# Transformer block (infini-attention and SwiGLU) on one core: first q and k by token quarters, and a table of priority shifts for the list scheduler

## The chip, the cores and the metric

The kernel runs on one core of a Trainium2 chip. The time is device microseconds of one execution. A run counts as fast when it is within 1.5% of the fastest of the same kernel. Differences in this study are below 1%, so next to the times I use a ledger of TensorE's own time, read from the trace matmul by matmul.

## The reference, cut to what matters

```python
x = A_x                                            # (1, 2048, 1024), bf16
h  = x + attention(layernorm(x), wq, wk, wv, wo, beta)   # 32 heads of 32
h2 = h + (silu(hn @ w1) * (hn @ w3)) @ w2                # hn = layernorm(h), F = 3584

# attention: 4 segments of 512 tokens, in order
for s in range(4):
    p   = softmax(qs @ ks.T * scale + mask)        # inside the segment
    mem = phi(qs) @ M / (phi(qs) @ z + 1e-6)       # from the segments before
    outs.append(g * mem + (1 - g) * (p @ vs))
    M, z = M + phi(ks).T @ vs, z + phi(ks).sum()
```

## The kernel before

The kernel builds a list of operations, each with a class, a place in the list (`seq`), dependences and a modelled cost. A list scheduler plays the list on a model of the engines and writes down an order for each engine; this order is what the chip runs. Each engine works through its order as written, so the scheduler decides who stands behind whom. A free engine takes the ready operation with the lowest (class, seq):

```python
def offer(o):
    o.offered = now
    for e in o.engs:
        heapq.heappush(avail[e], (o.cls, o.seq, o))
```

Matmuls of one accumulation form a group, which claims a PSUM bank when its first matmul is scheduled; from then on that matmul also depends on whoever had the bank last. A group marked `safe` asks for all its loads before its first matmul:

```python
if group.safe and group.ops:
    head = group.ops[0]
    for d, raw in list(o.deps.items()):
        if (not raw or d.kind == "dma") and d.seq < head.seq:
            self.dep(head, d, raw=raw)
```

Scores use one set of four banks, freed by one exponential on ScalarE (ACT). They run in a packed mode of TensorE (four matmuls of 32 rows); dense matmuls run in the full mode; the products with v in a column mode:

```python
def scores(self, s, parts):
    gr = self.queue(0, 1, 2, 3)
    ... 4 packed matmuls for each part, cls=0 ...
    self.g.op("act", act_ns(2048), ex, writes=[et[:, :, :]], cls=0, group=gr)   # exp
```

At the start, four row blocks of x are normalised, transposed on TensorE and copied to SBUF; the first q runs in two halves of 256 tokens so as not to wait for all four:

```python
def first_q(self, w):
    x = self.xnT[0]
    grs = [Group([(6,), (7,), (4,), (5,)], safe=True) for _ in range(4)]
    for half in range(2):
        c0 = 256 * half
        for i, gr in enumerate(grs):
            self.mms(gr, [(lambda gr, c0=c0: self.bank(gr, 0, 256, c0),
                           w[:, c, i * 128:(i + 1) * 128], x[:, c, c0:c0 + 256],
                           c == 0, c == 7, 256) for c in range(8)], 5, split=8, eager=True)
    for i, gr in enumerate(grs):
        self.evac(gr, self.qT[0][:, i, :], 512, lambda b: b, cls=1)
```

```python
self.g.dma(hr[:, :], self.hd[t * 128:(t + 1) * 128, :], cls=3)
...
gr = self.dense_group(True)                        # True: safe
self.mms(gr, [... 28 matmuls with hm[fc] and w2[fc // 4] ...], 8, eager=True)
self.g.op("dve", ..., reads=[hs], writes=[ob], cls=1, group=gr)   # ob = hs + bank
```

The softmax here doesn't subtract the row's maximum and nothing guards it: scores larger than these inputs give would overflow.

Of the kernel before, what the change touches and what calls it, by code (L numbers as in the profile page):

```python
# [13 lines left out]
ENGINES = ("pe", "act", "dve", "pool", "sp")  # L14


class Op:


    __slots__ = ("engs", "eng", "cost", "emit", "deps", "users", "cls", "seq", "missing",  # L20
                 "ready", "start", "end", "pos", "signal", "tok", "group", "first", "last",
                 "mode", "bytes", "kind", "snap", "gate", "port", "patience", "offered")

    def __init__(self, engs, cost, emit, cls, seq):
        self.engs, self.cost, self.emit, self.cls, self.seq = engs, cost, emit, cls, seq
        self.eng = None
        self.deps, self.users = {}, []
        self.missing = 0
        self.ready = 0.0
        self.start = self.end = None  # L30
        self.pos = None
        self.signal = False
        self.tok = None
        self.group = None
        self.first = self.last = False
        self.mode = None
        self.bytes = 0
        self.kind = None
        self.snap = None
        self.gate = None  # L40
        self.port = False
        self.patience = 0.0
        self.offered = 0.0


class Group:
# [23 lines left out]
class Graph:  # L70
# [9 lines left out]
    def __init__(self, nc, es):  # L80
        self.nc, self.es = nc, es
        self.ops = []
        self.pages = {}
        self.base = {}
        self.eng = {"pe": nc.tensor, "act": nc.scalar, "dve": nc.vector,
                    "pool": nc.gpsimd, "sp": nc.sync}
        self.bank_owner = [None] * 8
        self.bank_last = [[] for _ in range(8)]
        self.phase_left = {}


    def sbuf(self, name, shape, dtype, offset):
# [68 lines left out]
    def op(self, engs, cost, emit, reads=(), writes=(), cls=5, deps=(), group=None,  # L161
           kind=None, gate=None, port=False):
        if isinstance(engs, str):
            engs = (engs,)
        if not isinstance(cost, dict):
            cost = {e: cost for e in engs}
        o = Op(engs, cost, emit, cls, len(self.ops))
        o.kind = kind
        o.gate = gate
        o.port = port  # L170
        if gate is not None:
            self.phase_left[gate] = self.phase_left.get(gate, 0) + 1
        for ap in reads:
            self._touch(o, ap, False)
        for ap in writes:
            self._touch(o, ap, True)
        for d in deps:
            self.dep(o, d)
        o.group = group
        for group in (group.parts if isinstance(group, Both) else (group,) if group else ()):  # L180
            for prev in group.ops:
                if prev.engs != o.engs or o.engs != ("pe",):
                    self.dep(o, prev)
            if group.ops and o.engs == ("pe",):
                self.dep(o, group.ops[-1])
            o.first = not group.ops
# [5 lines that stand above are left out]
            group.ops.append(o)  # L192
            group.open += 1
        self.ops.append(o)
        return o
# [11 lines left out]
    def dma_t(self, out, in_, cls=5):  # L207
# [3 lines left out]
        o.bytes = 2 * 262144  # L211
        return o


    def schedule(self):
        ops = self.ops
        for o in ops:
            o.missing = len(o.deps)
            for d in o.deps:
                d.users.append(o)  # L220
# [250 lines left out]
class Kernel:  # L471
# [218 lines left out]

    def ln_act(self, k, src, dst):

        sm, nm, sq = (self.lnst[:, k, i:i + 1] for i in range(3))
        junk = self.oT[0][:, 0:2, :].rearrange("p a b -> p (a b)")
        G = self.g
# [13 lines left out]

    def ln(self, k, src, dst, cls):  # L710

        st = self.lnst[:, k, :]
        mv = self.lnmv[:, k, :]
        for c in range(2):
# [14 lines left out]
    def ln1(self, s):  # L729
        for i in range(4):  # L730
# [7 lines left out]
            if s:  # L738
# [6 lines left out]
            self.evac(gr, out, 1024, lambda b: b.rearrange("p (k n) -> p k n", k=8), cls=1,  # L745
                      bf=True)

    def qkv(self, s):
        p = s % 2
        for half in range(2):  # L750
            for kind in "qkv":
                n = self.n_wp
                self.n_wp += 1
                w = self.wp[n % 3]
                src = self.w[kind][:, half * 512:(half + 1) * 512].rearrange(
                    "(c p) n -> p c n", p=128)
                if n == 0:
                    self.g.dma(w[:, :, 0:256], src[:, :, 0:256], cls=1)
                    self.g.dma(w[:, :, 256:512], src[:, :, 256:512], cls=1)
                else:  # L760
                    self.g.dma(w[:, :, :], src, cls=1)
                if n == 0:
                    self.first_q(w)
                    continue
                for i in range(4):
                    gr = self.dense_group()
                    if kind == "v":
                        items = [(lambda gr: self.bank(gr), self.xnT[s][:, c, i * 128:(i + 1) * 128],
                                  w[:, c, :], c == 0, c == 7, 512) for c in range(8)]
                        out = self.v[p][:, i, half * 4:half * 4 + 4, 0:128]  # L770
                        view = lambda b: b.rearrange("p (g n) -> p g n", g=4)
                    else:
                        items = [(lambda gr: self.bank(gr), w[:, c, i * 128:(i + 1) * 128],
                                  self.xnT[s][:, c, :], c == 0, c == 7, 512) for c in range(8)]
                        out = (self.qT if kind == "q" else self.kT)[p][:, half * 4 + i, :]
                        view = lambda b: b
                    self.mms(gr, items, 5)
                    self.evac(gr, out, 512, view, cls=1)

    def first_q(self, w):  # L780

        x = self.xnT[0]
        grs = [Group([(6,), (7,), (4,), (5,)], safe=True) for _ in range(4)]
        for half in range(2):
            c0 = 256 * half
            for i, gr in enumerate(grs):
                self.mms(gr, [(lambda gr, c0=c0: self.bank(gr, 0, 256, c0),
                               w[:, c, i * 128:(i + 1) * 128], x[:, c, c0:c0 + 256],
                               c == 0, c == 7, 256) for c in range(8)], 5, split=8, eager=True)
        for i, gr in enumerate(grs):  # L790
            self.evac(gr, self.qT[0][:, i, :], 512, lambda b: b, cls=1)

    def phi(self, src, dst, cls):
        n = self.n_phi
        self.n_phi += 1
        e_, r = self.pe_e[0][:, :, :], self.pe_r[0][:, :, :]
# [14 lines left out]
    def memory(self, s, pr):  # L811

        p = s % 2
# [2 lines left out]
        self.phi(self.kT[p][:, 2 * pr:2 * pr + 2, :], pk[:, :, :], 4)  # L816
        pkn = self.pkn[pr % 2]
        self.g.dma_t(pkn[:, :, :], pk[:, :, :].rearrange("p a n -> p (a n)"), 3)
        gr = self.dense_group()
        items = []  # L820
        for a in range(2):
# [36 lines left out]
    def scores(self, s, parts):  # L858


        q, k = self.qT[s % 2], self.kT[s % 2]
        et = self.et[self.n_et % len(self.et)]
        self.n_et += 1
# [44 lines left out]
    def finish(self, s, g, pq, pieces):  # L908


        G = self.g
        v = self.v[s % 2]
        pm = (s - 1) % 2
        gm = self.queue(4) if s else None
# [13 lines left out]
        else:  # L928
            order = [(w, kc) for kc in range(4) for w in "nd"]
        both = Both(gn, gd)  # L930

        def emit(e, gr):
            ins = []
# [47 lines left out]
    def wo_stage(self, s):  # L981
        oT = self.oT[s % 2]
        for i in range(4):
            t = 4 * s + i
            h, hn = self.h[t % 3], self.hn[0]
            self.g.dma(h[:, :], self.x2d[t * 128:(t + 1) * 128, :], cls=2)
            for half in range(2):
                gr = self.dense_group(s >= 2)
                self.mms(gr, [(lambda gr: self.bank(gr), oT[:, c, i * 128:(i + 1) * 128],
                               self.wo[:, c, half * 512:(half + 1) * 512], c == 0, c == 7, 512)  # L990
                              for c in range(8)], 5 if s < 2 else 7)
                hs = h[:, half * 512:(half + 1) * 512]
                self.g.op("dve", dve_ns(512), lambda e, gr, hs=hs: [e.tensor_tensor(
                    hs, hs, self.bank(gr), op=ALU.add)], reads=[hs], writes=[hs], cls=1,
                    group=gr)
# [2 lines left out]
            self.g.dma_t(self.hnT[s][:, :, i * 128:(i + 1) * 128], hn[:, :], 2)  # L998

    def ffn_up(self, blk, ch):  # L1000
        n = self.n_w13
        self.n_w13 += 1
        w1, w3 = self.w13[n % 2]
# [3 lines left out]
        for jj in range(2):  # L1007
            fc = 2 * ch + jj
            for tc in range(2):
                hT = self.hnT[2 * blk + tc]  # L1010
                i = self.n_f % 2
                self.n_f += 1
# [18 lines left out]
    def ffn_down(self, blk):  # L1031
# [4 lines left out]
        for i in range(8):  # L1036
            t = 8 * blk + i
            hr = self.hr[t % 3]
            self.g.dma(hr[:, :], self.hd[t * 128:(t + 1) * 128, :], cls=3)
            cols = [(0, 512), (512, 256), (768, 256)] if t == 15 else [(0, 512), (512, 512)]  # L1040
            for c0, n in cols:
# [98 lines left out]
```

## Time and profile before

| | before |
|---|---|
| time, median of 3 runs | 913.40 us (913.02 to 914.52) |
| profiled span | 911.39 us |
| TensorE busy | 902.3 us, 99% |
| next busiest engine, VectorE | 434.3 us, 48% |
| matmuls, changes of tiling mode in the order | 5500, 209 |

A busy share of 99% says that TensorE is the bound, but not how much of its time is needed. The ledger does. I walked the matmuls in order of start. Each start-to-start distance is its columns at 2.4 GHz, plus 2.5 ns, plus 0.117 us if the mode changes, plus a rest; a rest over 0.06 us is a stall. In some traces 93 or 94 matmul records are missing, so every trace was first aligned with the order of the built program. The lines behind it are in the prediction.

### The profile page before, as it was taken

What the parts mean: (1) busy time and instruction counts of PE and PEld (TensorE: products, weight loads), DVE (VectorE), ACT (ScalarE), POOL (GpSimd) and SP (SyncE); (2) the same over time, 40 slices, a digit from 0 to 9 for tenths busy, and PEclk for the clock granted to TensorE, in tenths of its full rate; (3) what the DMA queues carried; (4) which work ended last, traced back from release to release, by engine and by line L of the source; (5) the groups of instructions that cost most, each with busy time, mean ns of one, the idle gap of its engine ahead of it and who ended that gap; (6) DMA issues with size and microseconds to landing.
All of it is one profiled execution on the core that took longest, in us unless ns stands there. A gap on an engine that the chain in (4) does not pass through costs nothing.

```text
span 911.4 us, 13038 instructions
## 1 busy us (share of the span) xinstructions
PE 902.3 (99%) x5500; PEld 406.1 (45%) x5500; DVE 434.3 (48%) x744; ACT 293.7 (32%) x310; POOL 175.0 (19%) x272
## 2 busy tenths in 40 slices
PE   8999999999999999999999999999999999999998
PEld 5444444444444344444444444444444444444445
DVE  3878878878767654544643411211343334431111
ACT  5877775776776611111111100000121111110000
POOL 3535655555454520100100000000000000000000
PEclk9999999999999999999999999999999999999999
DMA  9967753743543255823733211012133212301110
GB/s 313 243 173 188 174 137 100 186 132 94 137 107 104 71 203 155 190 65 104 191 74 93 66 51 47 24 37 79 49 96 93 70 46 70 93 24 41 35 42 29
DMA packets 145385, 96.26 MB, mean 106 GB/s; under 512 B 45360, under 2 KB 132528, under 8 KB 145328
## 3 DMA queue, kind: packets, MB, share of 16 engines
q1 hardware_dynamic: 145328, 95.45, 38.3%
q8 instruction: 43, 0.70, 0.3%
q14 instruction: 14, 0.11, 0.0%
HBM read 76.55 MB, written 8.39 MB: 93 GB/s over the span
## 4 chain that ended last, share of the span: by engine, by line
PE 97%; ACT 2%; DVE 1%; DMA 0%; issue 0%; SPq 0%
PE ps L598 90%; PE ps L939 4%; PE ps L871 3%; ACT et L884 1%; DMA xs<-in_A_x_dram 0%; DVE lnst L716 0%; DVE qT L622 0%; PE ps L610 0%; DVE xs L725 0%; SPq L203 0%; ACT v L621 0%; ACT qT L621 0%; DVE ob L1050 0%; DVE xs L707 0%; DVE lnmv L718 0%
## 5 line engine op out<-in xcount | busy, mean ns | idle before, releaser
L598 PE MATMUL ps<-hnT,w1b 128*128 128x512 bf16 x896 | 223.3, 379 | 0.3 <-DVE t L1022 0.3
L598 PE MATMUL ps<-hnT,w3b 128*128 128x512 bf16 x896 | 222.6, 379 | 0.0
L1019 ACT ACTIVATE sg<-ps 128x512 bf16<-128x512 f32 x112 | 66.9, 597 | 438.3 <-PE ps L598 434.7
L598 PE MATMUL ps<-w2b,hm 128*128 128x512 bf16 (+1 forms) x924 | 196.4, 373 | 0.0
L1022 DVE SCALAR_TENSOR_TENSOR t<-sg,ps 128x512 bf16<-128x512 bf16 x112 | 76.9, 686 | 213.3 <-ACT sg L1019 213.3
L884 ACT ACTIVATE et<-ps 128x2048 bf16<-128x2048 f32 x80 | 150.0, 1875 | 45.3 <-PE ps L939 23.1
L598 PEld LDWEIGHTS ps<-w2b,hm 128*128 128x128 bf16 x924 | 90.4, 98 | 103.3
L598 PEld LDWEIGHTS ps<-hnT,w1b 128*128 128x128 bf16 x896 | 87.0, 98 | 106.8 <-issue 7.8
L598 PEld LDWEIGHTS ps<-hnT,w3b 128*128 128x128 bf16 x896 | 87.4, 98 | 105.8 <-issue 0.8
L889 POOL TENSOR_SCALAR_AFFINE_SELECT et<-et 128x512 bf16<-128x512 bf16 x128 | 89.5, 716 | 116.9 <-ACT et L884 116.5
L1027 DVE SCALAR_TENSOR_TENSOR hm<-t,ps 128x512 bf16<-128x512 bf16 x112 | 76.9, 686 | 34.4 <-PE ps L598 31.2
L1050 DVE TENSOR_TENSOR ob<-hr,ps 128x512 bf16<-128x512 bf16 (+1 forms) x33 | 22.1, 671 | 143.1 <-PE ps L598 143.1
L598 PE MATMUL ps<-hnT,wp 128*128 128x512 bf16 x256 | 61.9, 380 | 0.3 <-DVE qT L622 0.3
L598 PE MATMUL ps<-xnT,wp 128*128 128x512 bf16 (+1 forms) x288 | 61.1, 356 | 0.3 <-DVE qT L622 0.3
L598 PE MATMUL ps<-wo,oT 128*128 128x512 bf16 x256 | 59.9, 379 | 0.0
L598 PEld LDWEIGHTS ps<-xnT,wp 128*128 128x128 bf16 x288 | 26.1, 98 | 26.7 <-issue 4.1
L598 PEld LDWEIGHTS ps<-wo,oT 128*128 128x128 bf16 x256 | 24.2, 98 | 29.9 <-issue 2.3
L598 PEld LDWEIGHTS ps<-hnT,wp 128*128 128x128 bf16 x256 | 23.1, 98 | 29.3 <-issue 4.6
L976 POOL TENSOR_TENSOR Nm<-Nm,R1b 128x512 f32<-128x512 f32 x23 | 29.6, 1289 | 20.2 <-DVE R1b L965 20.2
L871 PE MATMUL ps<-qT,kT 32*128 32x128 bf16 (+3 forms) x512 | 31.7, 301 | 1.8 <-ACT et L884 1.7
L950 DVE STREAM_TRANSPOSE T<-ps 128x512 f32<-128x512 f32 x32 | 22.9, 715 | 21.8 <-PE ps L939 21.5
L598 PE MATMUL ps<-wp,hnT 128*128 128x512 bf16 x128 | 31.1, 380 | 0.0
(84 smaller groups left out, 590.4 us busy)
## 6 DMA issues: line engine op xcount, KB each, us to landing
w1b<-in_B_w_dram SPq DMA_DIRECT2D x28, 512.0 KB, 3.9
w3b<-in_B_w_dram SPq DMA_DIRECT2D x28, 512.0 KB, 4.6
wp<-in_A_wk_dram SPq DMA_DIRECT2D x8, 1024.0 KB, 6.6
wp<-in_A_wv_dram SPq DMA_DIRECT2D x8, 1024.0 KB, 5.6
wp<-in_A_wq_dram SPq DMA_DIRECT2D x7, 1024.0 KB, 5.5
w2b<-in_B_w_dram SPq DMA_DIRECT2D x7, 1024.0 KB, 8.1
xs<-in_A_x_dram SPq DMA_DIRECT2D x16, 256.0 KB, 5.5
h<-in_A_x_dram SPq DMA_DIRECT2D x16, 256.0 KB, 4.1
```

What stands on the lines that cost most here:

```text
L598: return [e.matmul(p[0](gr), p[1], p[2], start=p[3], stop=p[4]) for p in part]
L871: ins.append(e.matmul(self.bank(gr, j, 512 - 128 * kc, off), k[r, g, 128 * kc:128 * kc + 128], q[r, g, 128 * kc:512], start=True, stop=Tru ...
L884: return [e.activation(et[:, :, :], src, AF.Exp, scale=self.scale)]
L889: self.pool_op(lambda e, m=m: e.affine_select(m, m, pattern=[[0, 4], [1, 128]], compare_op=ALU.is_ge, fill=0.0, base=0, channel_multiplier ...
L939: ins.append(e.matmul(self.ps[r, b * 512 + 128 * kc:(b + 1) * 512], lhsT, pieces[kc][:, j, :], start=kc == 0 and (what == "n" or s == 0), ...
L950: G.op("dve", dve_ns(512), lambda e, gr: [e.transpose(T1, self.bank(gr))], writes=[T1], cls=0, group=gd)
L976: self.either(lambda e: e.tensor_tensor(Nm, Nm, R1, op=ALU.mult), 512, 2, [Nm, R1], [Nm], 2)
L1019: self.g.op("act", act_ns(512), lambda e, gr, sg=sg: [e.activation(sg, self.bank(gr), AF.Tanh, scale=0.5)], writes=[sg], cls=2, group=gg)
L1022: e.scalar_tensor_tensor(t1, sg, 1.0, self.bank(gr), op0=ALU.add, op1=ALU.mult)], reads=[sg], writes=[t1], cls=2,
L1027: e.scalar_tensor_tensor(dst, t1, 0.5, self.bank(gr), op0=ALU.mult, op1=ALU.mult)], reads=[t1], writes=[dst], cls=2,
L1050: self.g.op("dve", dve_ns(n), lambda e, gr, hs=hs, ob=ob, n=n: [e.tensor_tensor(ob, hs, self.bank(gr, 0, n), op=ALU.add)], reads=[hs], wri ...
```

## The change

The intent: TensorE should work sooner, on quarters of the tokens of which the rows are ready, for two groups of q and two of k; the values come third. Then the order of the whole attention should have fewer waits: a table, found by search with the scheduler's engine model, moves stages of the list earlier or later.

```diff
+SHIFT = {
+    0: (-342, 0), 1: (-212, 0), 2: (315, 0), 3: (-6, 1), 4: (101, 1), 5: (384, 0), 6: (-38, -1),
...                                   (467 entries: shift of seq, shift of class)
     def schedule(self):
         ops = self.ops
+        for o in ops:
+            late, cls = SHIFT.get(o.unit, (0, 0))
+            o.seq += late + 1e-6 * o.seq
+            o.cls += cls
...
+    def stage(self):
+        self.unit += 1                # called at each layer norm, group, score block, ...
...
-    def first_q(self, w):             # two halves of 256 tokens, four groups of q
...
+    def first_half(self):
+        (wq, sq), (wk, sk), (wv, sv) = (self.weights(kind, 0) for kind in "qkv")
+        self.g.dma(wq[:, :, 0:256], sq[:, :, 0:256], cls=1)
+        self.g.dma(wk[:, :, 0:256], sk[:, :, 0:256], cls=1)
+        self.g.dma(wv[:, :, :], sv, cls=1)
+        self.g.dma(wq[:, :, 256:512], sq[:, :, 256:512], cls=1)
+        self.g.dma(wk[:, :, 256:512], sk[:, :, 256:512], cls=1)
+        work = [(w, i, Group([(6,), (7,), (4,), (5,)], safe=True))
+                for w in (wq, wk) for i in range(2)]
+        for c0 in range(0, 512, 128):
+            for w, i, gr in work:
+                self.g.stage()
+                self.mms(gr, [(lambda gr, c0=c0: self.bank(gr, 0, 128, c0),
+                               w[:, c, i * 128:(i + 1) * 128], x[:, c, c0:c0 + 128],
+                               c == 0, c == 7, 128) for c in range(8)], 5, split=8, eager=True)
...                                   (copies; then v; then the other two groups of q and of k)
```

## The prediction

> **What bounds the kernel now.** I read the page's busy shares first, then its chain, then the merged chain in order of time, and last the TensorE timeline of the first 60 us.
>
> ```profile
> PE 902.3 (99%) x5500; PEld 406.1 (45%) x5500; DVE 434.3 (48%) x744; ACT 293.7 (32%) x310; POOL 175.0 (19%) x272
> PE 97%; ACT 2%; DVE 1%; DMA 0%; issue 0%; SPq 0%
> ...
> 330.21 578.62 PE ps L598 x2708
> ```
>
> TensorE is busy for 99% of the span and is 97% of the chain that ended last. No other engine passes 48%. The last line is the feed-forward part: 2708 matmuls in one piece, with nothing ahead of any of them. So only TensorE's own time counts, and I split it. The built program's order lists 5500 matmuls. Without the 16 warm-up ones (3.4 us of columns), and with the four packed ones of the attention counted as one, their columns are 860.2 us at 2.4 GHz: 809.0 in full mode, 17.1 in the scores' row mode, 34.1 in the column mode of the value product. That cannot change. What remains of the span of 911.4 is 51.2 us, in five terms:
>
> - A fixed cost of a matmul. In the last piece 2652 matmuls of 512 columns and 56 of 256 are 571.7 us of columns and took 578.62: 6.9 / 2708 = 2.5 ns each. Over the 3948 full-mode ones after the warm-up: 9.9 us.
> - Changes of tiling mode, 209 in the order. Their price is in the timeline:
>
> ```profile
> 22.02 0.40 PE L871 MATMUL ps<-qT,kT 32*128 32x512 bf16 x4
> 22.35 2.76 PE L598 MATMUL ps<-xnT,wp 128*128 128x512 bf16 x12
> 25.05 0.40 PE L871 MATMUL ps<-qT,kT 32*128 32x128 bf16 x8
> ```
>
> (Columns: start, duration, engine, line, tiles, count.) Four packed score matmuls are 0.213 us of columns, and the next starts 0.33 later; twelve dense ones are 12 x 0.2158 = 2.59, and the next starts 2.70 later. That is 0.11 to 0.12 for a change in either direction, and the median over the attention part is 0.117. 209 x 0.117 = 24.4 us.
>
> - The head, up to the dense stream:
>
> ```profile
> 1.24 6.40 PE L598 MATMUL ps<-oT 128*128 128x512 bf16 x16 [1.24 <-DVE oT L652]
> 7.48 0.61 PE L610 MATMUL ps<-ident,xs 128*128 128x128 bf16 x8
> 9.23 0.61 PE L610 MATMUL ps<-ident,xs 128*128 128x128 bf16 x8 [1.14 <-ACT xnT L621]
> 10.46 0.62 PE L610 MATMUL ps<-ident,xs 128*128 128x128 bf16 x8 [0.62 <-DVE xs L725]
> 11.04 1.03 PE L598 MATMUL ps<-xnT,wp 128*128 128x256 bf16 x8
> 11.91 0.61 PE L610 MATMUL ps<-ident,xs 128*128 128x128 bf16 x8
> 12.36 9.73 PE L598 MATMUL ps<-xnT,wp 128*128 128x256 bf16 x72
> ```
>
> By 12.36 us TensorE has done 4 transposes of eight (1.71 us of columns) and one block of the first q (0.85). So 9.8 us of the head are no useful work; the bracket on the transposes shows the cause, the layer norm of the rows.
>
> - Stalls inside the attention. Where a start-to-start distance exceeds columns, 2.5 ns each and the change of mode, the excess sums to about 4.2 us. Most hang on the one set of four score banks, which is free only when the exponential (1.88 us) has read it:
>
> ```profile
> 35.92 0.23 PE L939 MATMUL ps<-et,ones 128*32 128x128 bf16 x4
> 36.65 0.39 PE L871 MATMUL ps<-qT,kT 32*128 32x512 bf16 x4 [0.50 <-ACT et L884]
> 36.97 1.90 PE L598 MATMUL ps<-xnT,wp 128*128 128x512 bf16 x8
> 39.02 0.40 PE L871 MATMUL ps<-qT,kT 32*128 32x128 bf16 x8 [0.15 <-ACT et L884]
> ```
>
> 36.65 to 39.02 shows the shortest round of this loop: 2.37 us from scores to scores, with eight dense matmuls too few to fill it.
>
> - The tail after the last matmul, about 2.6 us (the piece above ends at 908.83).
>
> The sum is 9.9 + 24.4 + 9.8 + 4.2 + 2.6 = 50.9 of the 51.2.
>
> **What the Trainium skill says.** "TensorE: Matmul & The Clock Gate", Part 1, gives a warm start-to-start of N / 2.4 GHz plus about 2.5 ns; this trace agrees (2.5 ns over 2708). The same page, LDWEIGHTS, puts a weight load at columns over 1.2 GHz, 107 ns, and Weight-path perf modes names a faster load for full bf16 weights. It matters here, because the change halves the moving columns to 128. The trace shows eight matmuls of 129 columns, each with new weights, from 43.81 to 44.36: 0.55 less one change of mode is 0.43, or 54 ns each, so columns bound it and not the load. "TensorEngine Tiling (Array Packing)", Key Properties, says that changing the tiling mode drains TensorE; the 0.117 us agrees. "Perfetto Trace Analysis", Identifying the Most-Contended Engine, warns that matmul busy time is a bad measure, and so it is: 99% busy hides 51 us.
>
> **The change part by part.**
>
> 1. First q, k. Before, all four groups of the first q come in two halves of 256 tokens. After it, two groups of q and two of k come in four quarters of 128, in the same four banks. For the first q and k together, 64 matmuls of 256 columns and 32 of 512 become 128 of 128 and 32 of 512. Columns are equal; 64 more instructions cost 64 x 2.5 ns = +0.16 us. A block (8 x 54 ns) is 0.43 us and needs only its own quarter of the rows. The timeline with all engines has the first quarter's copy to SBUF end at 9.14 us (ACT, 8.12 plus 1.02), so a block can run before the second transpose. In the after order blocks stand ahead of transposes 2 and 3 and three ahead of transpose 4, five in all. DVE, ACT and GpSimd have the same order in the layer norm as before. From 9.25 on, TensorE has then 3 transposes and 5 blocks, 3.4 us, and passes transpose 4 at about 12.7, not 12.36. Work done by then: 5 x 0.43 = 2.15 against 0.85; gain 1.3 less the 0.34 later, 1.0 us. Seven to eight blocks follow, over 3 us, more than the last quarter's copy (1.1 us) needs, so no new gap. This is near the limit: of 9.23 to 12.36 only 1.0 us was idle, and what lies before 9.2 waits for the rows in both.
> 2. q and k halves loaded as 512 KB pieces, values third. The first slice moves 313 GB/s, so rows (1 MB), q and k halves (0.5 MB each) are there by about 8 to 9 us (estimate from that rate). The k half is first needed near 11. Nothing gained or lost by itself.
> 3. The table shifts the priority of some 467 units. It adds no instruction. By the order, the changes of mode go from 209 to 206: -0.35 us. I also added up, in both orders, columns, 2.5 ns and 0.117 us between score blocks and compared with 2.37 us. Before, six rounds are too short, by 3.1 us in sum (0.86, 0.2, 0.2 around 36 to 41 us, then 0.2, 0.84, 0.84); after, two, by 1.3 (1.06 early in the first segment, 0.2 later). The true stalls before were 4.2 because of waits for copies too (two of 0.33 on the qT copy). Taking the same 1.1 us for those: 4.2 to about 2.8, gain 1.4 us.
>
> Sum: -1.0 + 0.16 - 0.35 - 1.4 = -2.6 us on the span.
>
> **The rivals.**
>
> - Weight loads come into the path. The table packs the users of a weight buffer closer to its next load. By the order, the shortest time between the last use of a projection buffer and the next first use falls from 17.2 us to 6.5 (twice, near 160 and 190 us), while such a load takes:
>
> ```profile
> wp<-in_A_wk_dram SPq DMA_DIRECT2D x8, 1024.0 KB, 6.6
> wp<-in_A_wv_dram SPq DMA_DIRECT2D x8, 1024.0 KB, 5.6
> wp<-in_A_wq_dram SPq DMA_DIRECT2D x7, 1024.0 KB, 5.5
> ```
>
> For: 6.5 is hardly above 5.5 and the queue issues in order, so a transpose waiting ahead of it can eat the rest. Against: the feed-forward's own shortest distance is 4.3 us with loads of 3.9 to 4.6 before, and nothing stalled. If it bites: one to two us at each of two or three places, and the result is 912 to 915.
> - The table fits its model and not the chip: other waits (copies out of the two dense banks, the row transposes) take the place of the removed ones. For: ACT must do gcol, three copies and one phi between the second and third exponential of the first segment. Against: there the order leaves 6.5 us between scores. If so, only the head's 1.0 and the 0.35 stay: 912.
> - The head gains more, as scores start near 17 us and not 22, and all stalls go: the cap is 1.0 + 0.35 + 4.2, so 908.
>
> **Range and chances.** The median of the timed runs, 913.4, is 2.0 above the profiled span. 913.4 - 2.6 = 910.8. All that the change can reach is 5.5 us, 0.6%, for 24.4 us of mode changes, 9.9 of fixed cost and 860 of columns stay. A loss needs new stalls, and 2% would be 18 us of them. So 907.8 to 913.6, with 0.01 for faster by over 2%, 0.98 within 2% and 0.01 slower.
>
> **What would show it.** The dense stream without gaps from about 9.3 us, and first scores near 17 us, show step 1. Equal distances of 0.117 at mode changes and 206 of them show step 3's first term. A sum of stalls near 2.8 us, with score waits on ACT mainly between the sixth and seventh score blocks, shows its second. The feed-forward piece must still run at 2.5 ns over columns. A TensorE wait on a load of wp or w1b would make the first rival right; a time outside 907.8 to 913.6, or a head gain over 2 us, would make my account wrong.

## The result, and the profile after

The changed kernel took 910.52 us in the median of 4 runs (910.06 to 911.80); the kernel before took 913.21 in the same rounds (912.89 to 914.52). The ratio is 0.997, with a 95% interval of 0.9953 to 0.9987. Ratios here are the mean time of one kernel's fast runs over that of the other's of the same rounds, so not quite the ratio of the medians quoted.

The profiled span fell from 911.39 to 908.58 us. From the page of the changed kernel, its busy times and its chain by engine:

```profile
PE 900.9 (99%) x5564; PEld 406.9 (45%) x5564; DVE 432.4 (48%) x742; ACT 293.0 (32%) x311; POOL 174.7 (19%) x273
PE 97%; DMA 1%; ACT 1%; DVE 0%; issue 0%; SPq 0%
```

There are 64 more matmuls, as planned. DMA has 1% of the chain where it had 0%: that is new. The last long piece of the chain (start, duration, what) is:

```profile
328.09 577.87 PE ps L697 x2704
```

It has 2704 matmuls in one piece, four fewer than before: 571.7 less 0.85 us of columns, and 2.6 ns each. So the feed-forward part is what it was, and the 2.8 us came from before 328 us. The timeline of TensorE in the head (start, duration, engine, line, operation, tiles, shapes, count, and in brackets the idle time before it and what ended it):

```profile
1.24 5.71 PE L697 MATMUL ps<-oT 128*128 128x512 bf16 x16 [1.24 <-DVE oT L751]
...
8.99 0.61 PE L697 MATMUL ps<-xnT,wp 128*128 128x128 bf16 x8 [1.21 <-ACT xnT L720]
...
11.25 1.50 PE L697 MATMUL ps<-xnT,wp 128*128 128x128 bf16 x24 [0.31 <-ACT xnT L720]
12.59 0.61 PE L709 MATMUL ps<-ident,xs 128*128 128x128 bf16 x8
13.03 3.74 PE L697 MATMUL ps<-xnT,wp 128*128 128x128 bf16 x64
...
17.57 0.40 PE L994 MATMUL ps<-qT,kT 32*128 32x512 bf16 x4
```

Blocks of 128 columns now stand among the transposes, and the first scores come at 17.57 us (22.02 before). But there is a second wait, at 11.25. In the attention, the longest waits of the same timeline are:

```profile
36.08 1.02 PE L697 MATMUL ps<-xnT,wp 128*128 128x512 bf16 x4 [0.43 <-ACT kT L720]
...
37.76 0.40 PE L994 MATMUL ps<-qT,kT 32*128 32x128 bf16 x8 [0.66 <-ACT et L1007]
...
174.36 1.04 PE L697 MATMUL ps<-hnT,wp 128*128 128x512 bf16 x4 [0.29 <-DMA wp<-in_A_wq_dram]
```

The last is a wait on a weight load, which the kernel before had nowhere on TensorE in its one profile. The ledger of both, from the first profile of each:

| term, us | before | after | difference | predicted |
|---|---|---|---|---|
| until the first transpose (idle and warm-up matmuls) | 7.48 | 7.17 | -0.31 | 0 |
| columns from there on | 860.09 | 860.09 | 0 | 0 |
| fixed cost of a matmul | 9.87 | 10.03 | +0.16 | +0.16 |
| changes of mode (209, 206) at 0.117 | 24.45 | 24.10 | -0.35 | -0.35 |
| stalls in the head | 2.22 | 1.85 | -0.37 | -1.0 |
| stalls in the attention | 4.93 | 2.82 | -2.11 | -1.4 |
| stalls in the feed-forward | 0 | 0.10 | +0.10 | 0 |
| last matmul to the end, and the sum of small rests | 2.35 | 2.42 | +0.07 | 0 |
| span | 911.39 | 908.58 | -2.81 | -2.6 |

The kernel before has this one profile. The changed one has four, and they show how far a term moves by itself: the attention's stalls are 2.4 to 3.0 us in them, so the fall from 4.93 is beyond that spread; the first line is 6.91 to 7.76 us, so its -0.31 is not.

### The profile page after: what moved, and what is told of

It reads as the page before. It is cut to its first block, busy times and chain, and to the rows that moved or that the text cites. A ratio compares the mean times of both kernels' runs of the same rounds, so it can differ in the third digit from the quotient of the medians.

```text
span 908.6 us, 13100 instructions
## 1 busy us (share of the span) xinstructions
PE 900.9 (99%) x5564; PEld 406.9 (45%) x5564; DVE 432.4 (48%) x742; ACT 293.0 (32%) x311; POOL 174.7 (19%) x273
## 4 chain that ended last, share of the span: by engine, by line
PE 97%; DMA 1%; ACT 1%; DVE 0%; issue 0%; SPq 0%
PE ps L697 90%; PE ps L1064 4%; PE ps L994 3%; DMA wp<-in_A_wq_dram 1%; ACT et L1007 1%; DMA xs<-in_A_x_dram 0%; ACT xnT L720 0%; PE ps L709 0%; SPq L294 0%; ACT kT L720 0%; DVE xs L826 0%; DVE ob L1180 0%; DVE lnst L817 0%
## 5 line engine op out<-in xcount | busy, mean ns | idle before, releaser
L697 PE MATMUL ps<-hnT,w1b 128*128 128x512 bf16 x896 | 219.5, 379 | 0.0
L697 PE MATMUL ps<-hnT,w3b 128*128 128x512 bf16 x896 | 219.0, 379 | 0.4 <-DVE t L1151 0.3
L697 PE MATMUL ps<-w2b,hm 128*128 128x512 bf16 (+1 forms) x924 | 199.0, 373 | 0.0
L697 PE MATMUL ps<-wo,oT 128*128 128x512 bf16 x256 | 62.5, 379 | 0.0
L823 POOL TENSOR_SCALAR lnve<-lnmv 128x1 f32<-128x1 f32 x31 | 8.3, 268 | 125.0 <-DVE lnmv L819 125.0
```

The costliest lines, as they stand in the source:

```text
L697: return [e.matmul(p[0](gr), p[1], p[2], start=p[3], stop=p[4]) for p in part]
L823: self.pool_op(lambda e: e.tensor_scalar(ve, var, self.EPS, None, op0=ALU.add), 1, [var], [ve], 0)
```

## The experiments

The theory was the prediction's: the gain is waits that went, in the head (quarters) and between score blocks (table). The rivals: only one half of the change pays; or the gain is larger and waits on loads take part of it back. After the first profile I added: the wait at 11.25 us is a PSUM bank and not missing rows.

### e0_again: the changed kernel unaltered

> The changed kernel unaltered, a second profile of it. By my account of the first profile (columns 860.1, fixed 11.1, 206 mode changes 22.6, stalls 4.8, warm-up 5.9, 1.2 before it, tail 2.9 us) everything but the warm-up repeats within 0.1 us: the stalls again 4.8 us at the same places, and the warm-up anything between 5.9 and 6.3, since its 16 matmuls ran partly at half clock and that end is not set by the program. Rival: the stalls differ by more than 0.5 us from profile to profile; then no single stall of a profile can be blamed for the gain. Time against the kernel before 0.996 to 0.998.

It took 910.72 us (910.24 to 911.57; before 912.97), ratio 0.9975 (0.9963 to 0.9988). The stalls of the head and the attention came at the same places (1.99 and 2.97 us). But the span was 909.41, above all because of one more wait of 0.77 us near 461 us in the feed-forward. All stalls sum to 5.73 us where the first profile has 4.77, so the rival of this expectation (over 0.5 us from profile to profile) came true: an order that never changes has waits that do. Two more runs of the same kernel, told below, showed the same. One such wait is in the head:

```profile
9.01 0.62 PE L697 MATMUL ps<-xnT,wp 128*128 128x128 bf16 x8 [1.35 <-DMA wp<-in_A_wq_dram]
```

In the first profile this block waited for the first quarter's copy. Here it waited 0.14 us longer, for the first half of wq, which was issued at 2.65 and landed 6.3 us later, at 8.95.

### e1_quarters: the quarters without the table

```diff
-SHIFT = {0: (-342, 0), ...}
+SHIFT = {}
```

> The changed kernel with an empty table: the quartered first q and k alone. Theory (my count on the order): 208 mode changes (-0.1 us), 64 more instructions (+0.15), head stalls 1.85 for 2.22 (-0.4), but the rounds between scores that are under 2.37 us sum to 4.0 us and not 3.1 (+0.8): +0.5 us on the span of before, 911.4 to 912.4, time ratio 1.000 to 1.001. Rival one, that the parts add: the head's gain alone, 0.8 us faster than before (912.5 in time, 0.999). Rival two, the kernel's own engine model, which has this version 1.5 us slower than before: 1.0017.

It took 914.12 us (913.86 to 914.24; before 912.89), ratio 1.001 (0.9998 to 1.0023); the median is 1.2 us above before. The span was 912.52, 0.1 above what was expected. The head's stalls were 1.85 us, as in the full change. But the stalls of the attention summed to 6.53 us. The largest, from the timeline:

```profile
35.28 0.39 PE L910 MATMUL ps<-qT,kT 32*128 32x512 bf16 x4
35.61 0.63 PE L613 MATMUL ps<-v,pkn 128*128 128x129 bf16 x8
37.81 0.40 PE L910 MATMUL ps<-qT,kT 32*128 32x128 bf16 x8 [1.57 <-ACT et L923]
```

Only eight short matmuls stand between two score blocks, and the round of the one set of score banks (2.53 us here) is paid as a wait. Here scores that start earlier, without new work to fill their rounds, gained nothing. Against this kernel the table is worth 3.6 us (914.12 to 910.52, in different rounds).

### e2_table: the table without the quarters

The first half is the old one; the table holds from stage 60 on. With the whole table on the old first half the scheduler found no order, so this is as much of it as can be tried.

```diff
-            late, cls = SHIFT.get(o.unit, (0, 0))
+            late, cls = SHIFT.get(o.unit if o.unit >= 60 else -1, (0, 0))
...
-    def first_half(self):
+    def first_q(self, w):             # as in the kernel before
```

> The old first half (first q by halves, then k, then v) with the table on everything from the second half on (units 60 and up; with all of it the scheduler deadlocks). Theory: 207 mode changes (-0.25 us), short score rounds 1.65 us in sum for 3.1 (-1.5 us), head as before: span 909.6 (0.998). Rival one, that the gain of the change sits in the first quarters: 911.4, no gain. Rival two, the engine model: 2.25 us faster than before, 909.1.

It took 913.24 us (912.31 to 914.14; before 912.89), ratio 0.9999 (0.9986 to 1.0013). Stalls of the attention: 4.35 us, and the waits of the first rounds stand where they stood before:

```profile
36.70 0.40 PE L999 MATMUL ps<-qT,kT 32*128 32x512 bf16 x4 [0.50 <-ACT et L1012]
...
41.45 0.40 PE L999 MATMUL ps<-qT,kT 32*128 32x256 bf16 x8 [0.15 <-ACT et L1012]
```

There were 207 changes of mode, and 0.86 us of wait on a w2b load near 463 us. The span was 911.49 where 909.6 was expected: the expectation failed, and so did the scheduler's model, which had 2.25 us of gain here. Without that wait some 0.8 us of gain on the span would be left (an estimate, 0.6 of stalls in the attention and 0.23 of mode changes). So each part alone gave nothing (+1.2 and +0.35 us by the medians), and both together give 2.7. The parts don't add up. That the table fits only the list for which it was searched is the likely reason; as it could not be tried in full on the other list, this is argued and not shown.

### e3_banks: the head's transposes in other banks

In the changed kernel the transposes' banks and the first q and k groups come from the same four. The orders of all engines stay; only the banks of the four transpose groups change, to those that the scores don't need yet.

```diff
+    def head_banks(self):                     # after schedule()
+        for o, p in self.g.by_bank:           # pairs noted when a bank is claimed
+            if p.group in self.head:
+                del o.deps[p]
+        first = next(o for o in self.g.order["pe"] if o.gate == "att")
+        for n, gr in enumerate(self.head):
+            gr.banks = (n,)
+            for o in gr.ops:
+                first.deps[o] = True
```

> The changed kernel with all orders kept, and only the four head transposes written to the score banks 0 to 3 in place of 4 to 7. Theory: the 0.48 us before the third row block (at 10.7 us) is the first k group waiting for a bank that a transpose's copy still holds, so head stalls fall from 1.85 to about 1.4 us, later waits shift with it, span 908.1. Rival: that block waits for its rows or for the k weights, or the time comes back at the next score wait; then the head stalls stay at 1.8 or the attention stalls grow from 2.9 to 3.4, and the span stays at 908.6.

The wait of 0.48 us was gone:

```profile
10.52 0.61 PE L711 MATMUL ps<-ident,xs 128*128 128x128 bf16 x8
10.96 1.50 PE L699 MATMUL ps<-xnT,wp 128*128 128x128 bf16 x24
```

The head's stalls were 1.40 us where the changed kernel has 1.85. So it was the bank: the first k group waited for a copy that still read it. But the time did not follow: 910.85 us (909.23 to 911.18), ratio 0.997 (0.9956 to 0.9983), level with e0_again. The profile shows where it went: TensorE arrived 0.6 us earlier at the first w2 group, and waited there 1.38 us, until 461.07; e0_again waited until 461.06. The wait ended at the same time whenever TensorE came. That looks like a transfer.

### e4_rows and e5_early: two attempts on what was left

e4_rows adds to e3_banks a shorter way for the first row: VectorE normalises row block 0 ahead of the first statistics of block 2, and 12 warm-up matmuls take the place of 16.

```diff
+        dve[i - 1], dve[i] = apply, stats      # on VectorE's order
-        ... * 16, 0, split=16)
+        ... * 12, 0, split=12)
```

> As e3_banks, with the first row's normalisation put ahead of the third row's first statistics on VectorE, and 12 warm-up matmuls in place of 16. Theory: the head is bound by the rows, so the first transpose starts about 0.35 us earlier than in e3 (near 6.7 to 6.8 us) and the span falls by another 0.3 us, to 907.8. Rival: later rows come 0.2 us later on VectorE and take it back (change under 0.1 us), or fewer warm-up matmuls leave the clock low and the first blocks run at half speed (over 1 us slower).

It took 911.79 us (910.07 to 911.87), ratio 0.9983 (0.997 to 0.9995). The first transpose came 0.24 us earlier than in the first profile after (6.93), but the third, whose row was put back, waited 0.41 us. Up to the dense stream, warm-up and stalls sum to 7.50 us against 7.48 in e3_banks: nothing gained. The first block could hardly have come earlier still, since the wq load landed at 2.65 + 6.1 = 8.75, just before it started (8.78). The span was 910.12 and not 907.8, for later waits of 0.98 us near 174 (a wq load), 0.55 near 423 and 0.78 near 634 us. The profile puts the last down to a w3b load; the one near 423 was not traced further.

e5_early adds to e4_rows the removal of the wait at 36 us: banks 6 and 7 change places from the q group that waited on, and the second half of that group runs ahead of the scores.

```diff
+                    x.banks = (13 - x.banks[0],)
...
+        pe.remove(second)
+        pe.insert(pe.index(scores), second)
```

> As e4_rows, with the dense banks 6 and 7 exchanged from the first q of the second half on, and the second half of that q group moved ahead of the seventh scores. Theory: the 1.2 us of stall around 36 us (0.49 for the bank, 0.70 for the exponential) shrink to about 0.3, a new one of 0.3 comes before the eighth scores, span 0.6 us under e4: 907.2. Rival: the weights of that q, asked for at 28.1 us, land too late for it, or the exponential's round of 2.4 us sets all scores in that stretch whatever stands between; then the span equals e4's within 0.15 us.

It took 911.83 us (909.95 to 912.38), ratio 0.9982 (0.9969 to 0.9994). The two waits of 0.49 and 0.70 us became three, of 0.32, 0.60 and 0.17, in the next rounds:

```profile
39.09 0.40 PE L999 MATMUL ps<-qT,kT 32*128 32x128 bf16 x8 [0.27 <-ACT et L1012]
...
41.80 0.40 PE L999 MATMUL ps<-qT,kT 32*128 32x256 bf16 x8 [0.55 <-ACT et L1012]
42.51 1.67 PE L699 MATMUL ps<-xnT,wp 128*128 128x512 bf16 x7 [0.32 <-ACT qT L722]
```

1.19 us became 1.09. In this one try, moving a block only changed where the wait of the score rounds was paid.

The span of 910.10 equals e4's, as the rival said, but partly by chance. The first block came at 9.15, after the wq load (2.65 + 6.5), and then the granted clock was 0.50 from 10 to 13 us; by the distances of the matmuls this cost about 1.6 us. It is what e4's rival had feared of fewer warm-up matmuls. e4's own profile, with the same 12, doesn't have it, so the cause stays open.

### e6_loads and e7_after: the load behind the wait at 461 us

With this order a w2b load (1 MB) is issued near 452 us, right behind three loads of hr (0.75 MB; the block of the residual that VectorE adds at the end of a w2 group) that nobody reads until 547. e6_loads takes e3_banks, puts those three behind six later issues, and moves two pieces of TensorE's work ahead of the group that waited near 174 us.

```diff
+        del sp[at:at + 3]                      # hr, hr, hr
+        sp[at + 6:at + 6] = hr
...
+        pe[i:i + 3] = [phi, scores, q]         # was [q, scores, phi]
```

> The kernel with its head transposes in banks 0 to 3 (e3_banks), and two orders edited. On the DMA queue, the three loads of hr (0.75 MB, first read near 547 us) stand behind six later issues, so that the 1 MB load of w2b near 452 us has no 0.75 MB ahead of it. On TensorE, the matmul with Mbf and the four scores that followed the q group near 174 us stand ahead of that group, which waited for its weights by 0.19 to 0.98 us in five profiles. Theory A (the waits near 174 and 461 us are transfers of weights that arrive late): the w2b load is there in under 7.5 us from its issue (7.6 to 9.0 before), the stall near 461 us (0.8 and 1.4 us in two of three profiles with this order) is below 0.1, the one near 174 us is below 0.3, the sum of the feed-forward's stalls is below 0.3, and the span is 907.5 to 908.8 us, against 909.4 of both repeats. Theory B (the wait at 461 us, whose releaser the profile calls issue, is not that load): the stall near 461 us stays at 0.8 or more in about two of three profiles and the span stays at 909 to 910. In both the timed median moves by no more than 1.5 us against the changed kernel on the same chip, 0.2%, so the stalls in the trace decide, not the time.

It took 917.76 us (917.55 to 918.11; before 912.87), ratio 1.0051: 7 us slower than the changed kernel. My edit had made things worse; the trace says how. The DMA queue's timeline, and TensorE's:

```profile
451.79 0.37 SPq L295 DMA_DIRECT2D w2b<-in_B_w_dram  x1
...
459.86 1.81 SPq L295 DMA_DIRECT2D hr<-h_scr  x3
```

```profile
458.50 1.03 PE L699 MATMUL ps<-hnT,w1b 128*128 128x512 bf16 x4
465.60 1.86 PE L699 MATMUL ps<-w2b,hm 128*128 128x512 bf16 x4 [6.07 <-issue]
467.25 1.91 PE L699 MATMUL ps<-hnT,w1b 128*128 128x512 bf16 x4
```

The w2b load itself did what theory A says. Its line in the list of DMA issues (tensor, engine, size, us from issue to landing) is:

```profile
w2b<-in_B_w_dram SPq DMA_DIRECT2D x1, 1024.0 KB, 5.8
```

It landed at 457.6, before TensorE came. But the wait lasted until 465.60, and the first of the three hr loads was issued at 459.86; they land in 5.6 us in the median, 465.5. The group is marked safe, so its first matmul asks for every load of the group, hr among them, although only VectorE reads that. In the kernel as it was, hr was there long before and this wait could not be seen. So neither theory was right for this run: A's transfer was confirmed, and its span of 907.5 to 908.8 failed because the edit made a second wait. And there was a second price: after 6 us of idle time the next matmuls took 0.43 us each instead of 0.216. In the window 465 to 470 us the granted clock was 0.50, and 2.4 us were lost on top of the 6.2. The Trainium skill ("TensorE: Matmul & The Clock Gate", Part 1) says that TensorE falls to half rate after an idle window of about 3.4 us; the 6.07 us here agree, and the 1.38 us at this place in e3_banks did not do it. But in the head of e5_early the clock fell to half although no single wait was over 1.6 us, so the length of one wait does not settle it.

The unaltered kernel in the same rounds:

> The changed kernel unaltered, once more, on the same chip as e6_loads and beside the same runs of the kernel before, so that both are compared in the same rounds. Theory A: 910.3 to 911.5 us in the median, 0.9970 to 0.9985 of before, waits on weights near 174 us again (0.2 to 1.0) and near 461 us in some profiles (0 to 1.4), and e6_loads ahead of it by 0.5 to 1.5 us. Theory B: the same for this kernel, and e6_loads level with it within 0.4 us.

It took 910.72 us (910.58 to 911.33), ratio 0.9975 (0.9963 to 0.9988). No wait near 174 us this time, and 1.04 us near 460. Timeline and load:

```profile
460.51 1.02 PE L697 MATMUL ps<-w2b,hm 128*128 128x512 bf16 x4 [0.88 <-issue]
```

```profile
w2b<-in_B_w_dram SPq DMA_DIRECT2D x1, 1024.0 KB, 8.5
```

It was issued at 451.89, so it landed at 460.4: the wait that the profile puts down to "issue" ends when this load lands. In no profile with hr in front does the group start before that landing, and where it stalls, it starts within 0.11 us of it (a landing is the issue plus the time to landing, added up from the two views):

| profile | w2b lands at | first matmul starts at | stall |
|---|---|---|---|
| first after | 452.65 + 7.3 = 460.0 | 460.23 | 0 |
| e0_again | 452.71 + 8.3 = 461.0 | 461.06 | 0.77 |
| e3_banks | 452.11 + 8.9 = 461.0 | 461.07 | 1.38 |
| e4_rows | 453.39 + 7.5 = 460.9 | 460.98 | 0 |
| e5_early | 453.89 + 6.4 = 460.3 | 461.47 | 0 |
| e7_after | 451.89 + 8.5 = 460.4 | 460.51 | 1.04 |

### e8_apart and e9_after: the load in front, and hr waited for by its reader alone

e8_apart is e6_loads without TensorE's waits on hr; VectorE keeps its own, so nothing is read too early.

```diff
+        for o in self.g.order["pe"]:
+            for d in [d for d in o.deps if d.kind == "dma" and d.bytes == 262144]:
+                if 467 <= o.unit and d.unit >= 467:
+                    del o.deps[d]
```

> The kernel of e6_loads, which was slower because the first matmul of a w2 group, marked safe, waits for every load that its group touches, the hr block of its result too, though only VectorE reads that some 90 us later. Here those waits of TensorE on hr loads are dropped (VectorE keeps its own); the order of the loads is that of e6_loads. Theory A (the 0.6 to 1.4 us near 461 us was the w2b load behind three hr loads, and the 6.2 us of e6_loads was the hr load alone): the w2b load lands within 6.3 us of its issue, the stall near 460 us is below 0.1 and no matmul after it runs at half the clock, the feed-forward's stalls sum to less than 0.3, the span is 907.3 to 908.3. The time is 0.5 to 1.8 us below the changed kernel in the same rounds. Theory B (something other than these two loads held that group): a stall of 0.5 us or more stays near 460 us and the span is 908.5 or more.

It took 909.49 us (909.24 to 909.58; before 913.32), ratio 0.9956 (0.9944 to 0.9969), with a span of 907.51. The w2b load took 6.1 us, and nothing waits:

```profile
458.30 1.03 PE L699 MATMUL ps<-hnT,w1b 128*128 128x512 bf16 x4
459.16 1.03 PE L699 MATMUL ps<-w2b,hm 128*128 128x512 bf16 x4
```

The feed-forward's stalls are 0.00, those of the head 1.37, of the attention 2.49 (0.13 of it at 174 us). Theory A holds in every number. It was tested by taking hr out of the way; what sets the time of a landing was not.

> The changed kernel unaltered, in the same rounds as e8_apart. By theory A 910.3 to 911.3 us in the median, 0.997 to 0.9985 of before, with the stall near 461 us between 0 and 1.4 us, as far as the landing of the w2b load (7.3 to 8.9 us after its issue) lies behind TensorE's arrival at 460.2 or earlier; by theory B the same, and e8_apart within 0.4 us of it.

The changed kernel took 910.37 us (910.10 to 910.63) in the same rounds, ratio 0.9966 (0.9952 to 0.9979), with a span of 908.91; its w2b load landed at 452.98 + 7.4 = 460.4, just before 460.56, and it waited 0.21 us near 174. The five runs of e8_apart all lie below its five; by the means it is 0.1% faster (909.42 against 910.41). It is the best of all kernels run, if by little. Its edits were not tried one by one. Of the 1.40 us between these two spans, 0.76 lies before the first transpose (chance), 0.47 is the head's bank, 0.08 the wait near 174 and 0.08 the feed-forward. So in this pair the load cost nothing; what e8_apart takes away is the 0.77 and 1.04 us that came in other profiles. The load in ring order is what the Trainium skill ("DMA: Bandwidth & Descriptors", Queues, rings and completion order) describes: on each DMA engine, descriptors of one issuing engine are taken in ring order. The runs agree: 5.8 and 6.1 us without the hr loads in front, 6.4 to 8.9 behind their 0.75 MB.

## Why the prediction was right

The time came within 0.3 us of the predicted one (910.52 and 910.8), but not all by the right terms.

- **What bounds the kernel.** Right. TensorE is 97% of the chain in both, and columns, fixed cost and mode changes came out as worked out: +0.16 and -0.35 us.
- **Step 1, the head: -1.0.** Right in kind, too large: -0.37 us of stalls. The step said that from 9.25 us on the dense stream would have no gaps. It has one of 0.48 us, since a transpose's copy still held the bank that the first k group took (e3_banks: with other banks the head gives -0.82). I had counted rows and matmuls, and not who holds the four banks. The 0.31 us before the first transpose can't be called an effect of the change: the same kernel's four profiles have 7.17, 7.05, 6.91 and 7.76 us there, and the same 16 warm-up matmuls took 6.40 us before and 5.71 after.
- **Step 2, the loads in halves: 0.** Not quite. Rows and halves were to be there by 8 to 9 us. The wq half landed between 8.15 and 9.04 us in the four profiles, and in e0_again it held the first block for 0.14 us. The wk half landed at 10.6 in the first one (3.12 + 7.5), 0.6 us before its first use. The order of the loads was not tested alone.
- **Step 3, the table: -1.4 on stalls.** Right in kind, too small, and the working has a slip: short score rounds of 1.3 us and 1.1 us of other waits make 2.4 after, not 2.8, and so a gain of 1.8, not 1.4. The total would then have been -3.0. The attention's stalls went from 4.93 to 2.82, 2.97, 2.37 and 2.58 us in four profiles. For before I had 4.2, 0.7 less than the ledger; I did not trace where my first count lost it. The figure for after, 2.8, was met by luck, for its parts are not as foretold. By a second walk of both traces (4.85 and 2.80 in sum) the waits of score blocks went from 2.13 to 0.90 us, where 3.1 and 1.3 were reckoned, and the other waits from 2.72 to 1.90, where 1.1 was to stay. So before, most of the stalls did not hang on the score banks. The waits at 36 and 37.8 us stand between the sixth and seventh score blocks, as foretold. What the step did not see is that the table, as far as it could be tried alone, gained nothing in time: e2_table still has 4.35 us of these stalls, and the quarters alone have 6.53. I had summed the two parts as if each had its own gain.
- **First rival, loads come into the path: partly true.** I had taken the projection buffers near 160 and 190 us as the danger, at one to two us a place. One such wait exists, at 174 us, of 0.45, 0.60, 0 and 0.21 us in the four profiles. A larger one came where I had not looked, in the feed-forward, where before had no stall: 0.77 and 1.04 us in two of the four, by the landing of one w2b load. (The 0.10 and 0.08 of the other two stand near 415 us, before another group.) Together the waits on loads take 0.2 to 1.4 us back, differently in each run.
- **Second rival, the table fits its model only.** Not true for the whole change: the scheduler's model says 916.9 before and 912.5 after, a gain of 4.4, and the chip gave 2.7. But of e2_table it said 2.25 us faster, and the chip gave nothing.
- **Third rival, 908.** Not reached by the changed kernel. e8_apart, with the bank, the load and the order near 174 us mended, comes to 909.5.

So the mechanism was right, but that the total came so close is luck: the head was put 0.6 us too high, the stalls of the attention 0.7 too low, and 0.3 us came by chance before the first transpose. Still open are why the same w2b load behind the same loads takes 7.3 us in one run and 8.5 in another, what halved the clock in e5_early's head, and how much of the table's gain hangs on which of its 467 entries.

## What to carry to other kernels

A table of priorities found for one list of operations is part of that list: test it with the change it was found for, and don't sum the gains of the halves. When one engine is full to 99%, follow each saved microsecond to the end: earlier arrival at a load that lands at a fixed time gives nothing. Look also at what the first instruction of a group waits for: a wait that asks for more than its own operands costs nothing until someone moves a load.

## What the Trainium skill lacked or had wrong

- "TensorEngine Tiling (Array Packing)", Key Properties, says that a change of mode drains TensorE, but not what it costs: 0.117 us each here, 206 to 209 times, 24 us of 911.
- "TensorE: Matmul & The Clock Gate", Back-to-back issue gap, gives 131 ns for a sustained stream of weight loads and matmuls at 512 columns, and 81 ns at 128. The runs show 215.9 ns (2704 matmuls in 577.87 us, 56 of them of 256 columns) and 56 ns (64 matmuls with new weights from 13.03 to 16.61 us). The formula that the page gives for single matmuls is the one that holds.
- "DMA: Bandwidth & Descriptors", Queues, rings and completion order, gives the order but no price of standing behind other loads: a 1 MB load took 5.8 and 6.1 us in front of 0.75 MB, 6.4 to 8.9 behind it, and up to 1.2 us more or less from run to run in one unchanged order.
- No page that I read says that a wait which the profile puts down to "issue" can be a load: the ones near 461 us (0.60 to 1.22 us by the profile) ended within 0.11 us of the landing of a w2b load.
